# Five small changes in a fused windowed-attention and wave-MLP kernel: value sums, a mixing piece, a weight transpose and a pair of masks put at other places, six fills given to GpSimd

## Chip, cores, metric

The kernel runs on one core of a Trainium2 chip. The metric is the device time of one execution in microseconds (us), lower is better. Times are medians of several executions. All comparisons use fast runs only (runs that are not slowed by a lower TensorE clock; the granted clock is the share of full speed that the profile records for TensorE). A profile is one execution, recorded by the hardware profiler; its span is some 1.8 us shorter than the device time of the same run.

Engine names in the profile: PE is TensorE's matmuls, PEld its weight loads, DVE VectorE, ACT ScalarE, POOL GpSimd, SP the engine that issues most DMA. L267 is line 267 of the kernel file. In the lines by time, the first number is the start in us from the begin of the span, the second the duration in us. Brackets give how long the engine stood idle just before, and what ended that.

## The reference, cut to what matters

```python
# attention: q, k, v are (B=4, H=8, S=768, D=64); 4 sink keys, window of 128
scores = q @ k^T / sqrt(D)
keep   = (key < 4) | ((row - key >= 0) & (row - key < 128))
a      = softmax(where(keep, scores, -1e9))
x      = (a @ v), heads merged: (4, 768, 512)

# wave MLP on x
theta = x @ w_theta
zr, zi = x * cos(theta), x * sin(theta)
u   = x + w_tok_r @ zr + w_tok_i @ zi      # mixing over the 768 tokens
out = u + relu(u @ w_ch)
```

The kernel works on *pairs* of heads, 4 per batch, 16 in all (pair 0 to 3 are batch 0). For one pair: transposes of q and k on PE, three groups of scores (0, 1, 2), exp on ScalarE, a mask product on VectorE for some groups, value sums on PE (called avp or av), division on VectorE (x_nat), transposes of x (xtp). Once a batch of x is there: theta sums (thp), sines on ScalarE (cs), products zz on VectorE, mixing sums (yp) by pieces of three matmuls, u, transposes of u, channel sums (wp), output. While batch b does attention, batch b-1 does its mixing, as filler. In batch 0 there is no filler, and the mixing weights themselves must be transposed on PE (wtp) before they can be used.

## The kernel before: the parts concerned

The order of TensorE, ScalarE, GpSimd and of the DMA queue is the order of the program text; VectorE's is left to a scheduler for batch 0 and is the text's order from batch 1 on.

```python
cast   = pool("cast", 2)                       # q, k in bf16, two buffers each
ps_sc  = pool("ps_sc", 2, space=PSUM)          # scores, thetas: two buffers
ps_sm  = pool("ps_sm", 2, space=PSUM)          # all transposes: two buffers
ps_mm  = pool("ps_mm", 2, space=PSUM)          # mixing and channel sums, first value sums
...
def later_constants():                         # cleared places for later sink values
    nc.vector.memset(vsf, 0.0)                 # 128 x 1024 fp32
    nc.vector.memset(rows, 0.0)
    for tb in range(NB):
        nc.vector.memset(rows[32 * tb:32 * tb + NS, tb:tb + 1], 1.0)
...
# batch 0
for i in range(HP):                            # HP = 4 pairs
    scores(i, 0)
    if i < HP - 1:
        next_heads(i, "q")                     # transposes of the next pair's q
    if i >= 2:
        weigh(i - 2, 0)                        # value sums of a pair, first head
    scores(i, 1)
    if i < HP - 1:
        next_heads(i, "k")
    if i >= 2:
        weigh(i - 2, 1)
    scores(i, 2)
    cast_v(i)                                  # GpSimd: v to bf16
...
wtok_transposes(0, 1)
cast_qk(HP)
mix(0, 0, 0, 4)                                # first mixing sums of block 0
thetas(0, 2)
wtok_transposes(1, 0)                          # weights of block 1
wtok_transposes(1, 1)
cast_wtok(2)
pool_copy(wch[:, 0:2, :], wch_f[0])            # GpSimd: channel weights to bf16
pool_copy(wch[:, 2:4, :], wch_f[1])
...
mix(0, 1, 10, 12)
mixed.append((0, 1))
turn()                                         # transposes of u, block 0
next_heads(HP, "q")
finish()                                       # channel sums and output, block 0
# batch 1
def slot(i, blk, wtok=None):
    ...
    if first:
        ...
        piece(blk, 0)                          # three mixing matmuls of block blk
        piece(blk, 1)
    ...                                        # scores, transposes, more pieces
    if hp > 0:
        weigh(i - 1, 0)
        weigh(i - 1, 1)
    finish()
...
# end of batch 1 (i = 7, its last pair)
five = (p, 5)
mask_product(i, 1)                             # VectorE: two products on E
mask_product(i, 2)
piece(five, 0)
x_transposes(b, HP - 2)                        # third part of x
next_heads(i, "q")
piece(five, 1)
weigh(i, 0)                                    # needs both masks
next_heads(i, "k")
weigh(i, 1)
theta_sums(b, 0, (0, 1))
x_transposes(b, HP - 1)                        # fourth part of x
```

The softmax here doesn't subtract the row's maximum and nothing guards it: scores larger than these inputs give would overflow.

## Time and profile before

| kernel before | |
|---|---|
| device time, median of 4 runs | 184.84 us (184.02 to 185.56) |
| span of the profile | 182.6 us |
| PE busy | 168.3 us, 92% |
| PE idle at the four waits that the change names | 2.50 us |

The chain of work that ended last, in the kernel before (start, duration, what):

```profile
5.57 9.20 DMA vf<-in_v_dram
14.85 1.24 POOL vx L76
16.13 0.50 PE avp L267 x11
```

The values of pair 0 land at 14.8, GpSimd casts them, and only then do the value sums go. ScalarE feels it too, since the next scores stand behind those sums:

```profile
17.43 1.02 ACT L231 ACTIVATE E<-sc 128x1024 bf16<-128x1024 f32 x1 [1.52 <-PE sc L218]
```

### The profile page before, as it was taken

To read this page: it belongs to the slowest core of one execution; us is meant where nothing else is said; L and a number is where in the kernel's file an instruction comes from. 1 tells how busy PE (TensorE), PEld (TensorE's weight loads), DVE (VectorE), ACT (ScalarE), POOL (GpSimd) and SP (SyncE) were. 2 spreads that over 40 slices of the span, in tenths; PEclk is the share of its full clock that TensorE was granted. 3 is DMA by queue.
4 is the path that set the end of the run, shared out by engine and by line. 5 is a ranking of instruction groups with operands and counts; after the bars stand their busy time and mean duration, and the time that the engine had idled before them with its cause. 6 is when DMAs were issued, how large, how long until landed. Compare 5 with 4: busy or idle time off the path is not lost.

```text
span 182.6 us, 4057 instructions
## 1 busy us (share of the span) xinstructions
PE 168.3 (92%) x1617; PEld 90.3 (49%) x1643; DVE 119.8 (66%) x221; ACT 103.0 (56%) x112; POOL 70.6 (39%) x95
## 2 busy tenths in 40 slices
PE   7897997998999988998999999999999999999991
PEld 2444573553466666443565554434555544344560
DVE  6686776792758589377596892686868825824451
ACT  4796778527886683799956801798454029300000
POOL 8987388987751632315584000563000000000000
PEclk9999999999999999999999999999999999999997
DMA  6999999999993899990839765995574530133413
GB/s 176 311 306 258 349 393 408 384 370 341 340 339 134 216 297 288 212 241 15 160 66 165 168 114 148 282 291 143 130 117 102 129 90 0 57 96 105 140 66 115
DMA packets 69907, 36.81 MB, mean 202 GB/s; under 512 B 57984, under 2 KB 64384, under 8 KB 69888
## 3 DMA queue, kind: packets, MB, share of 16 engines
q1 hardware_dynamic: 68592, 36.38, 72.4%
q0 software_dynamic: 1152, 0.04, 0.6%
q8 instruction: 13, 0.21, 0.5%
q10 hardware_dynamic: 144, 0.13, 0.2%
q14 instruction: 6, 0.05, 0.1%
HBM read 25.82 MB, written 6.29 MB: 176 GB/s over the span
## 4 chain that ended last, share of the span: by engine, by line
PE 64%; ACT 10%; DVE 9%; DMA 8%; issue 4%; SPq 2%; POOL 1%; DVEq 0%; ACTq 0%
PE yp L362 25%; PE thp L320 10%; PE wp L390 9%; PE avp L267 5%; DMA vf<-in_v_dram 5%; PE sc L218 5%; SPq L117 2%; DVE zz L333 2%; ACT cs L330 2%; PE tp L192 2%; ACT cs L329 2%; DMA xT<-x_nat 2%; ACT E L231 2%; PE wtp L347 2%; PE xtp L297 2%
## 5 line engine op out<-in xcount | busy, mean ns | idle before, releaser
L231 ACT ACTIVATE E<-sc 128x1024 bf16<-128x1024 f32 x48 | 47.5, 1028 | 14.7 <-PE sc L218 13.5
L362 PE MATMUL yp<-zz,wiT 128*128 128x512 bf16 x133 | 50.4, 379 | 1.3 <-issue 0.8
L362 PE MATMUL yp<-zz,wrT 128*128 128x512 bf16 x131 | 49.7, 380 | 2.0 <-DVE zz L333 1.7
L333 DVE TENSOR_TENSOR zz<-cs,x_nat 128x1024 bf16<-128x1024 bf16 x24 | 21.0, 913 | 14.6 <-ACT cs L330 14.6
L76 POOL TENSOR_SCALAR q<-qf 128x768 bf16<-128x768 f32 x14 | 13.3, 950 | 42.6 <-DMA qf<-in_q_dram 21.9
L237 DVE TENSOR_TENSOR E<-E,mask 128x768 bf16<-128x768 bf16 (+1 forms) x27 | 23.7, 915 | 2.8 <-ACT E L231 2.2
L366 DVE TENSOR_TENSOR u<-yp,x_nat 128x512 bf16<-128x512 f32 x23 | 15.8, 689 | 12.9 <-PE yp L362 12.1
L390 PE MATMUL wp<-wch,uT 128*128 128x512 bf16 x84 | 22.3, 379 | 0.9 <-DVE uT L383 0.5
L320 PE MATMUL thp<-wth,xT 128*128 128x512 bf16 x93 | 22.5, 379 | 0.3
L393 DVE SCALAR_TENSOR_TENSOR of<-wp,u 128x512 f32<-128x512 f32 x23 | 15.8, 685 | 9.4 <-PE wp L390 8.9
L329 ACT ACTIVATE cs<-thp,half_pi 128x1024 bf16<-128x1024 f32 (+1 forms) x13 | 13.6, 1050 | 14.7 <-PE thp L320 14.6
L362 PEld LDWEIGHTS <-wiT 128*128 128x128 bf16 x138 | 13.5, 98 | 14.9 <-issue 2.0
L362 PEld LDWEIGHTS <-wrT 128*128 128x128 bf16 x138 | 13.5, 98 | 13.3 <-issue 1.7
L267 PEld LDWEIGHTS <-E 128*128 128x128 bf16 x480 | 17.1, 97 | 4.9 <-issue 1.2
L218 PE MATMUL sc<-qT,kT 64*128 64x256 bf16 x192 | 16.6, 264 | 1.8 <-ACT kT L196 0.8
L273 DVE TENSOR_TENSOR x_nat<-avp,rec 128x384 bf16<-128x384 f32 x27 | 15.0, 557 | 0.9
L76 POOL TENSOR_SCALAR vx<-vf 128x768 bf16<-128x768 f32 x16 | 14.0, 883 | 1.9 <-DMA vf<-in_v_dram 1.9
L76 POOL TENSOR_SCALAR k<-kf 128x768 bf16<-128x768 f32 x14 | 12.9, 920 | 4.6 <-issue 2.4
L320 PEld LDWEIGHTS <-xT 128*128 128x128 bf16 x96 | 9.1, 98 | 10.7 <-DVE xT L302 0.6
L218 PEld LDWEIGHTS <-kT 64*128 64x128 bf16 x192 | 6.4, 94 | 15.4 <-issue 11.5
L267 PE MATMUL avp<-vx,E 128*128 128x65 bf16 x297 | 13.2, 193 | 0.7 <-POOL vx L76 0.7
L419 ACT COPY lT<-ltp 128x256 bf16<-128x256 bf16 x2 | 0.7, 372 | 21.2 <-PE ltp L417 21.2
(79 smaller groups left out, 206.6 us busy)
## 6 DMA issues: line engine op xcount, KB each, us to landing
qf<-in_q_dram SPq DMA_DIRECT2D x16, 384.0 KB, 5.6
kf<-in_k_dram SPq DMA_DIRECT2D x16, 384.0 KB, 5.8
vf<-in_v_dram SPq DMA_DIRECT2D x16, 384.0 KB, 4.9
out_dram<-of SPq DMA_DIRECT2D x23, 256.0 KB, 2.4
wf<-in_moe_w_tok_r_dram SPq DMA_DIRECT2D x6, 384.0 KB, 6.6
wf<-in_moe_w_tok_i_dram SPq DMA_DIRECT2D x6, 384.0 KB, 7.8
sqf<-in_moe_w_theta_dram SPq DMA_DIRECT2D x2, 512.0 KB, 6.3
sqf<-in_moe_w_ch_dram SPq DMA_DIRECT2D x2, 512.0 KB, 8.1
```

Of the source, the lines that this page charges most:

```text
L76: nc.gpsimd.tensor_scalar(out=out, in0=in_, scalar1=1.0, scalar2=1.0, op0=ALU.mult, op1=ALU.mult)
L218: nc.tensor.matmul(sc[:, e, 256 * part:256 * part + n], lhsT=kT[r, m * P:(m + 1) * P], rhs=qT[r, m * P:m * P + n], start=not biased, stop= ...
L231: nc.scalar.activation(out=E[:, :, 512 * c:512 * (c + 1)], in_=sc, func=AF.Exp, scale=SCALE)
L237: nc.vector.tensor_tensor(out=E[:, :, r], in0=E[:, :, r], in1=mask2[:, :, r], op=ALU.mult)
L267: nc.tensor.matmul(avp[:, t, :], lhsT=lhsT, rhs=rhs, start=(j == 0), stop=(j == len(seq) - 1), skip_group_check=True)
L320: nc.tensor.matmul(th_t[b, g][:, st, :], lhsT=xT[:, cb, 2 * g + st, :], rhs=wth[:, cb, :], start=(cb == 0), stop=(cb == NC - 1))
L329: nc.scalar.activation(out=cs[:, part, 0, :], in_=thp[:, part, :], func=AF.Sin, bias=half_pi)
L333: nc.vector.tensor_tensor(out=z_t[b][:, 2 * g + st, :, :].rearrange("p o (c n) -> p o c n", c=HP), in0=cs[:, st, :, :].rearrange("p o (c n ...
L362: nc.tensor.matmul(yp, lhsT=wT[i][:, t, sc, :], rhs=z_t[b][:, sc, i, :], start=(j == 0), stop=(j == 2 * NT - 1))
L366: nc.vector.tensor_tensor(out=u.rearrange("p (c n) -> p c n", c=HP), in0=yp.rearrange("p (c n) -> p c n", c=HP), in1=x_t[b][:, :, t, :], o ...
L390: nc.tensor.matmul(wp, lhsT=uT[:, cb, :], rhs=wch[:, cb, :], start=(cb == 0), stop=(cb == NC - 1))
L393: nc.vector.scalar_tensor_tensor(out=of, in0=wp, scalar=0.0, in1=u, op0=ALU.max, op1=ALU.add)
```

## The change

Its intent: put ready work of TensorE in front of work that must wait, in four places, and take some memsets from VectorE.

```diff
--- before.py
+++ after.py
@@ -487,10 +487,10 @@
         nc.vector.memset(low, -30000.0)
 
     def later_constants():
-        nc.vector.memset(vsf, 0.0)
-        nc.vector.memset(rows, 0.0)
+        nc.gpsimd.memset(vsf, 0.0)
+        nc.gpsimd.memset(rows, 0.0)
         for tb in range(NB):
-            nc.vector.memset(rows[32 * tb:32 * tb + NS, tb:tb + 1], 1.0)
+            nc.gpsimd.memset(rows[32 * tb:32 * tb + NS, tb:tb + 1], 1.0)
 
     def make_mask():
         ones = struct.unpack("f", struct.pack("I", 0x3F803F80))[0]
@@ -549,7 +549,8 @@
                 next_heads(i, "q")
             if i >= 3 * HP:
                 scores(i, 0)
-            piece(blk, 0)
+            if i > HP:
+                piece(blk, 0)
             piece(blk, 1)
         if pending:
             wtok_transposes(pending.pop(), 1)
@@ -588,6 +589,9 @@
         if hp > 0:
             weigh(i - 1, 0)
             weigh(i - 1, 1)
+        if i == 2 * HP - 1:
+            mask_product(i, 1)
+            mask_product(i, 2)
         finish()
         if wtok is not None:
             pending.append(wtok)
@@ -624,9 +628,11 @@
         scores(i, 0)
         if i < HP - 1:
             next_heads(i, "q")
-        if i >= 2:
+        if i > 2:
             weigh(i - 2, 0)
         scores(i, 1)
+        if i == 2:
+            weigh(i - 2, 0)
         if i < HP - 1:
             next_heads(i, "k")
         if i >= 2:
@@ -657,9 +663,9 @@
     phases(0, 1)
     wtok_transposes(0, 1)
     cast_qk(HP)
+    wtok_transposes(1, 0)
     mix(0, 0, 0, 4)
     thetas(0, 2)
-    wtok_transposes(1, 0)
     wtok_transposes(1, 1)
     cast_wtok(2)
     pool_copy(wch[:, 0:2, :], wch_f[0])
@@ -681,6 +687,7 @@
     mixed.append((0, 1))
     turn()
     next_heads(HP, "q")
+    piece((0, 2), 0)
     finish()
 
 
@@ -721,8 +728,6 @@
             piece(five, 1)
         else:
             five = (p, 5)
-            mask_product(i, 1)
-            mask_product(i, 2)
             piece(five, 0)
             x_transposes(b, HP - 2)
             next_heads(i, "q")
```

It has five parts, called A to E below. **A**: later sinks cleared by GpSimd. **B**: value sums of pair 0 (its first head) behind pair 2's second scores. **C**: one weight transpose ahead of the first mixing sums. **D**: the first mixing piece of block 2 ahead of the first channel sums (and no longer in slot 4). **E**: masks of pair 7 ahead of the output step of block 4, which stands in `finish()`.

## The prediction, written before the changed kernel ran

> **What bounds the kernel now.** I read the page first, then the chain of work that ended last, then the waits and the instructions in order of time around each line that the diff touches. The page's busy table says that TensorE is the engine to look at, and the slices say that its throttle grants it nearly full speed throughout, so only its idle time and its order matter:
>
> ```profile
> PE 168.3 (92%) x1617; PEld 90.3 (49%) x1643; DVE 119.8 (66%) x221; ACT 103.0 (56%) x112; POOL 70.6 (39%) x95
> PE   7897997998999988998999999999999999999991
> ...
> PE 64%; ACT 10%; DVE 9%; DMA 8%; issue 4%; SPq 2%; POOL 1%; DVEq 0%; ACTq 0%
> ```
>
> PE is 92% busy and holds 64% of the chain. Its thin slices lie in the first 45 us, and the diff works mostly there. In order of time, TensorE waits there at four places that the change names (start, duration, then the idle time before it and its releaser):
>
> ```profile
> 16.13 0.50 PE L267 MATMUL avp<-vx,E 128*128 128x65 bf16 x11 [0.73 <-POOL vx L76]
> ...
> 30.70 0.38 PE L362 MATMUL yp<-zz,wrT 128*128 128x512 bf16 x1 [0.64 <-DVE zz L333]
> ...
> 41.73 1.04 PE L390 MATMUL wp<-wch,uT 128*128 128x512 bf16 x3 [0.46 <-DVE uT L383]
> ...
> 72.15 0.27 PE L267 MATMUL av<-vx,E 128*128 128x65 bf16 x3 [0.67 <-DVE E L237]
> ```
>
> The reader is to see four different waits, all before instructions that the diff moves: the first pair's value sums wait for the GpSimd cast of values that land late; the first mixing sums wait for the products zz; the first channel sums wait for the copy of a transpose; the last pair of batch 1 waits for its mask. Added, they are 2.50 us, 1.4% of the time. What the change can win is about that.
>
> **What the Trainium skill says.** "TensorE: Matmul & The Clock Gate", section "Step-by-step: what each phase is for": only weight loads are pulled ahead, matmuls stay in program order. So a waiting matmul holds all later ones, and moving a ready group in front of it is free. The trace agrees: in the 0.73 us nothing else ran on PE, though the next scores had all they needed (below). "SBUF — State Buffer", section "Who interferes with whom": a VectorE instruction with two SBUF inputs contends with a GpSimd instruction that reads SBUF, and the first to issue blocks the other; one that only writes does not contend. The trace agrees on the first half:
>
> ```profile
> 69.18 0.68 DVE L393 SCALAR_TENSOR_TENSOR of<-wp,u 128x512 f32<-128x512 f32 x1
> 69.78 1.22 DVE L237 TENSOR_TENSOR E<-E,mask 128x2048 bf16<-128x2048 bf16 x1
> ...
> 70.55 1.14 POOL L76 TENSOR_SCALAR q<-qf 128x768 bf16<-128x768 f32 x1 [5.21 <-PE tp L192]
> ...
> 70.91 1.18 DVE L237 TENSOR_TENSOR E<-E,mask 128x768 bf16<-128x768 bf16 x1
> ```
>
> The 128x768 mask product, whose shortest record is 0.55 us, took 1.18 beside that cast, and the cast 1.14 instead of 0.83. "GPSIMD Engine Reference", section "3. Performance versus the Vector engine", warns that GpSimd is slower per element; for a memset this case's own 128x704 fill took 0.68 us, and that is what I use.
>
> **Part by part.**
>
> *Later sinks cleared by GpSimd.* VectorE loses a memset of 0.91 us at 4.34, one of 0.06 and four small ones (0.37). It gains no time on the path: after them it waits 1.16 us for the second query's DMA anyway, and the first scores at 7.99 follow ScalarE, which starts the mask's bias at 5.08 when GpSimd has made the mask, then copies qT and kT until 7.93. An earlier cast of k changes neither. GpSimd gets 1024/704 x 0.68 = 0.99 us, plus five small fills (those at the start are issued 0.03 us apart but last 0.10): about 1.3 us. They go behind the fourth value cast, which ends at 19.82, where GpSimd idles 2.10 us until a weight lands at 21.92. Hidden. **0 us.**
>
> *Value sums of pair 0 behind the second scores of pair 2.* Before, PE ends the transposes of pair 3's q at about 15.12, issues four sink products, waits to 16.13, does the sums and starts those scores at 16.47. They need a scores buffer whose exp ended near 14.9 (three exps start at 12.85, 1.02 each), so they can start at 15.12. They last 0.86 us (16.47 to 17.32) and end at 15.98; the cast of the values ends at 16.09; so the sums start with practically no wait. Everything behind them gains 0.73. ScalarE gains more at once: its exp waited 1.52 us until 17.43 and can now start when the exp before it ends, 15.91, plus some 0.1. VectorE takes up kT of pair 3 about 0.5 us sooner, which just keeps pace with the scores that need it. Later suppliers have slack: the third and fourth values are cast by 19.82 and used after 22; the theta weights by 24.27 and needed at 25.9. **0.7 us.**
>
> *A weight transpose ahead of the first mixing sums.* Six transposes, 0.34 us, leave a busy stretch at 34.1 and go into the 0.64 us wait. The compiled order shows VectorE's copy of it (0.47) now between the second product and the third, where VectorE waits 0.45 for ScalarE. But the gain is not all kept: at 37.19 the next weight transpose needs the PSUM buffer that ScalarE's copy of qT frees at 36.99, only 0.20 earlier; that copy follows the sines of the third theta group, which does not come earlier by this part. So 0.34 shrinks to about **0.15 us**.
>
> *A mixing piece ahead of the first channel sums.* Three matmuls of 0.216 spacing, 0.65 us, go into a wait that the trace gives as 0.46; counting the pipelined tail of the transposes before it (six at 0.056 from 40.77 end their issue at 41.11), PE stands for 0.62. The piece fills it; the channel sums start where they did, and the piece is gone from behind them. Its sum buffer is free once the first u is formed (40.48). **0.6 us.**
>
> *Masks of pair 7 ahead of the output of block 4.* VectorE swaps one 0.60 us step with two mask products. PE's 0.67 wait goes, but PE then meets VectorE again at 74.12, where the last transposes of x wait for x_nat. VectorE runs without a pause from 69.18 to 74.07, and a swap inside does not shorten that. What does is the contention: the small product would run from 70.3 to 70.9, starting before the cast at 70.55, and keep its 0.55 instead of 1.18. That is **0.6 us** if the order of issue turns so, and 0.05 if not; I take 0.45.
>
> Sum: 0 + 0.7 + 0.15 + 0.6 + 0.45 = **1.9 us**. Behind it the waits are mostly relative (PE, ScalarE and VectorE waiting for each other), and the loads have slack: the casts in batch 1 wait for PE's transposes to free a buffer more than for DMA. So I expect most to reach the end, and take 0.1 off for a wait that reforms: 184.6 - 1.8 = **182.8 us**.
>
> **Rivals.**
> - *VectorE is the bound at the end of batch 1.* Then the mask swap gives 0.05 and only some 1.4 us remain: 183.2. For it: VectorE's unbroken run to 74.07, while PE arrives at 74.10. Against it: the contended 1.18.
> - *Transfers bound the first batch.* DMA engines are over 90% busy in nearly all slices to 50 us. If the value and weight loads set the pace, the first gain is handed back and the total is about 0.8: 183.8. Against it: casts of q, k and weights for batch 1 end 4 to 10 us ahead of their transposes.
> - *A new wait takes the place of an old one.* With the mixing piece ahead, channel sums of block 1 take the buffer that u of block 2 must leave; u begins at 46.81 and lasts 0.69, and those sums start at 47.5 to 47.7. That is even, worth 0.2 at most. GpSimd's fills could delay the weights if each took several times the estimate: 0.8 us of slack stand against it.
> - *Everything is kept, and contention falls elsewhere too* (zz lasts 1.30 beside a cast, 0.84 alone): 182.0.
>
> **Range and chances.** The rivals span 182.0 to 183.8. The three runs before span 1.5 us, so medians may be off by 0.4 on either side: 181.8 to 184.0. Faster by over 2% needs 180.9, more than the four waits together: 4%. Slower by over 2% would need 3.7 us of new waits, for which I see no cause: 1%. Within 2%: 95%.
>
> **What would show it.** Right: value sums of pair 0 near 16.0 with no wait of 0.7, ScalarE's idle 1.52 gone; x transposes near 21.5 instead of 22.21; the first channel sums near 40.9 with no wait, mixing right behind; av without its 0.67, and a 128x768 mask near 0.55; theta sums of batch 1 starting about 1.9 earlier than 73.30 to 75.28. Wrong: the value sums still waiting for GpSimd; a weight wait longer than 2.10 or moved behind the fills; PE waiting about 0.6 for x_nat near 73; an end that moved much less than the start of batch 2 did.

## More of the kernel before

Since TensorE keeps its order within each kernel, the run can be cut into six stretches by the starts of seven PE instructions. The busy time by stretches of the kernel before (first two numbers: the stretch and its length; then busy us and count of PE, PEld, DVE, ACT and POOL; then the granted clock, the DMA share and GB/s):

```profile
core 0: us, PE busy (x) PEld busy (x) DVE busy (x) ACT busy (x) POOL busy (x), PEclk, DMA share, GB/s
7.99:22.21 14.22, 12.60 (x189) 6.86 (x193) 10.76 (x23) 10.94 (x11) 9.52 (x13) 1.00 1.12 306
22.21:41.73 19.52, 17.62 (x197) 10.96 (x191) 15.24 (x25) 12.10 (x16) 17.69 (x19) 1.00 1.06 387
41.73:43.99 2.26, 2.21 (x9) 0.89 (x10) 0.69 (x1) 1.65 (x2) 2.26 (x3) 1.00 1.15 348
43.99:69.56 25.57, 24.14 (x309) 14.89 (x314) 16.96 (x32) 18.88 (x22) 11.90 (x16) 1.00 0.90 273
69.56:74.12 4.56, 3.82 (x55) 2.65 (x54) 4.41 (x8) 2.06 (x3) 2.36 (x3) 1.00 1.16 279
74.12:178.71 104.59, 101.37 (x843) 51.22 (x857) 66.20 (x112) 52.38 (x55) 19.60 (x22) 1.00 0.57 131
```

The cuts are: first scores; first transposes of x; first channel sums; first scores of batch 1; third part of x of batch 1; fourth part of x; last matmuls. Idle PE is small everywhere, and the waits that the change names lie in the first, second, third and fifth stretch. (PE counts differ by a few between profiles, since some matmul records are missing from a trace; starts are not affected.)

## The result

| | before | changed |
|---|---|---|
| first measurement, median | 184.84 us, 4 runs | 182.30 us, 4 runs (182.03 to 182.62) |
| second measurement, on chip 10 | 184.82 us, 11 runs | 182.49 us, 5 runs (181.72 to 182.62) |
| ratio, first | | 0.9864, 95% interval 0.9818 to 0.9910 |
| ratio, second | | 0.9853, 95% interval 0.9822 to 0.9885 |

A ratio is the mean time of the changed kernel's fast runs over that of the other kernel's fast runs of the same rounds, so it is not quite the ratio of the medians. The change gains 1.4 to 1.5%, about 2.5 us: clear of noise. The point prediction was 182.8.

The stretches of the changed kernel's first profile, by the same seven instructions:

```profile
8.01:21.45 13.44, 13.01 (x193) 6.83 (x193) 10.36 (x19) 10.97 (x11) 10.55 (x16) 1.00 1.11 295
21.45:40.83 19.38, 18.38 (x201) 11.11 (x194) 15.44 (x25) 12.13 (x16) 17.21 (x20) 1.00 1.06 386
40.83:42.44 1.61, 1.61 (x9) 0.59 (x9) 0.55 (x1) 1.59 (x2) 1.42 (x3) 1.00 1.14 328
42.44:68.00 25.56, 24.57 (x314) 14.87 (x314) 17.55 (x33) 18.93 (x23) 14.81 (x18) 1.00 0.97 297
68.00:71.94 3.94, 3.77 (x56) 2.56 (x55) 3.79 (x8) 2.35 (x3) 2.52 (x3) 1.00 0.69 175
71.94:176.41 104.47, 102.70 (x856) 51.20 (x857) 66.11 (x112) 52.12 (x55) 19.54 (x22) 1.00 0.62 136
```

Stretch by stretch the gain is 0.78, 0.14, 0.65, 0.01, 0.62 and 0.12 us, 2.32 in all, less 0.02 for a later start: 2.30, which is the difference of the spans (182.6 and 180.3). The four places of the prediction, in the changed kernel's lines by time:

```profile
16.15 1.02 ACT L231 ACTIVATE E<-sc 128x1024 bf16<-128x1024 f32 x1 [0.17 <-PE sc L218]
16.20 0.50 PE L267 MATMUL avp<-vx,E 128*128 128x65 bf16 x11
...
29.68 0.38 PE L362 MATMUL yp<-zz,wrT 128*128 128x512 bf16 x1
...
40.83 1.03 PE L390 MATMUL wp<-wch,uT 128*128 128x512 bf16 x4
...
69.44 0.50 PE L267 MATMUL av<-vx,E 128*128 128x65 bf16 x11
```

None of the four has an idle time ahead of it any more, and ScalarE's 1.52 us are 0.17. What TensorE now waits for in batch 0 between 25 and 42 us is this:

```profile
30.91 0.38 PE L362 MATMUL yp<-zz,wrT 128*128 128x512 bf16 x1 [0.37 <-DVE zz L333]
34.84 0.39 PE L362 MATMUL yp<-zz,wiT 128*128 128x512 bf16 x1 [0.30 <-DVE wiT L351]
```

The first was there before. The second is new: a wait for VectorE's copy of the other weight transpose, which stood behind two products zz. It takes back part of what the transpose moved into the first wait had gained; the second stretch gained only 0.14 in this profile (more under "C alone").

The masks of part E, with the cast that disturbed them before:

```profile
67.63 1.68 DVE L237 TENSOR_TENSOR E<-E,mask 128x2048 bf16<-128x2048 bf16 x2
68.76 0.55 DVE L237 TENSOR_TENSOR E<-E,mask 128x768 bf16<-128x768 bf16 x1
68.99 1.01 POOL L76 TENSOR_SCALAR q<-qf 128x768 bf16<-128x768 f32 x1 [5.23 <-PE tp L192]
```

Before, both mask products together took 2.31 us. The small one (the second line, which is the tail of the first) now starts 0.23 us before the cast and takes 0.55 instead of 1.18; the cast is the one that is lengthened.

And the fills of part A on GpSimd:

```profile
19.09 1.23 POOL L76 TENSOR_SCALAR vx<-vf 128x768 bf16<-128x768 f32 x1 [0.58 <-DMA vf<-in_v_dram]
20.27 0.94 POOL L490 MEMSET vsf<- 128x1024 f32 x1
21.16 0.09 POOL L491 MEMSET rows<- 128x4 f32 x1
21.31 0.48 POOL L493 MEMSET rows<- 4x1 f32 x4
21.87 2.06 POOL L76 TENSOR_SCALAR wth<-sqf 128x1024 bf16<-128x1024 f32 x2
```

They take 1.52 us, and the weight casts follow at once. GpSimd did not wait for the weights' DMA here, so they may have landed before the fills ended. Nothing was lost, since the theta sums that use the first weights start at 24.67.

### The profile page after: what moved, and what is told of

Its sections match the earlier page's. It is cut to its first block, busy times and chain, and to the rows that moved or that the text cites.

```text
span 180.3 us, 4084 instructions
## 1 busy us (share of the span) xinstructions
PE 169.7 (94%) x1643; PEld 89.4 (50%) x1643; DVE 118.5 (66%) x215; ACT 103.1 (57%) x112; POOL 73.3 (41%) x101
## 4 chain that ended last, share of the span: by engine, by line
PE 66%; ACT 15%; DVE 8%; DMA 3%; issue 2%; POOL 2%; DVEq 0%; ACTq 0%; POOLq 0%
PE yp L362 25%; PE wp L390 9%; PE thp L320 9%; PE sc L218 6%; PE avp L267 6%; ACT E L231 3%; ACT cs L329 3%; ACT cs L330 3%; DVE zz L333 3%; PE tp L192 3%; DMA xT<-x_nat 2%; PE sc L211 2%; PE wtp L347 2%; PE xtp L297 2%; DVE x_nat L273 1%
## 5 line engine op out<-in xcount | busy, mean ns | idle before, releaser
L362 PE MATMUL yp<-zz,wrT 128*128 128x512 bf16 x138 | 52.4, 380 | 0.9 <-DVE zz L333 0.6
L362 PE MATMUL yp<-zz,wiT 128*128 128x512 bf16 x138 | 52.3, 379 | 0.6 <-DVE wiT L351 0.3
L390 PE MATMUL wp<-wch,uT 128*128 128x512 bf16 x92 | 23.6, 379 | 0.1
L76 POOL TENSOR_SCALAR k<-kf 128x768 bf16<-128x768 f32 x14 | 13.6, 970 | 4.6 <-DMA kf<-in_k_dram 2.5
```

Source lines behind the costliest of these rows:

```text
L76: nc.gpsimd.tensor_scalar(out=out, in0=in_, scalar1=1.0, scalar2=1.0, op0=ALU.mult, op1=ALU.mult)
L362: nc.tensor.matmul(yp, lhsT=wT[i][:, t, sc, :], rhs=z_t[b][:, sc, i, :], start=(j == 0), stop=(j == 2 * NT - 1))
L390: nc.tensor.matmul(wp, lhsT=uT[:, cb, :], rhs=wch[:, cb, :], start=(cb == 0), stop=(cb == NC - 1))
```

## The experiments

Twelve runs were made, of eleven kernels (the changed one and ten variants). Each was correct and was timed in five rounds beside the kernel before on the same chip. The medians below come from three chips, so the ratios are what can be compared. Since the fast runs of one kernel span 0.6 to 2.6 us (in the profiles, part of it is when the first loads land), the totals of parts worth 0.6 us have wide intervals. The stretches of the profiles are the sharper instrument, because each part lies in one stretch. All profiles of fast runs, with the length of stretches 1 to 6 in us:

| kernel (parts in it) | first scores at | 1 | 2 | 3 | 4 | 5 | 6 | median us | ratio to before (95%) |
|---|---|---|---|---|---|---|---|---|---|
| before | 7.99 | 14.22 | 19.52 | 2.26 | 25.57 | 4.56 | 104.59 | 184.8 | 1 |
| b_only (B) | 7.99 | 13.39 | 19.32 | 2.27 | 25.56 | 4.57 | 104.63 | 183.49 | 0.9950 (0.9916 to 0.9984) |
| c_only (C) | 7.99 | 14.23 | 19.00 | 2.27 | 25.56 | 4.57 | 104.60 | 183.95 | 0.9956 (0.9930 to 0.9982) |
| d_only (D) | 8.87 | 14.13 | 19.52 | 1.60 | 25.57 | 4.57 | 104.60 | 184.58 | 0.9984 (0.9956 to 1.0011) |
| e_only (E) | 7.99 | 13.87 | 19.48 | 2.26 | 25.57 | 3.94 | 104.47 | 184.21 | 0.9962 (0.9939 to 0.9985) |
| no_e (ABCD) | 8.01 | 13.39 | 18.86 | 1.60 | 25.57 | 4.57 | 104.65 | 182.87 | 0.9921 (0.9886 to 0.9957) |
| no_e_cast3 | 8.01 | 13.92 | 19.35 | 1.61 | 25.89 | 4.50 | 104.47 | 183.25 | 0.9939 (0.9900 to 0.9978) |
| no_e_dve10 | 8.01 | 13.60 | 18.81 | 1.61 | 25.66 | 3.87 | 104.65 | 182.82 | 0.9889 (0.9844 to 0.9934) |
| changed (ABCDE) | 8.01 | 13.44 | 19.38 | 1.61 | 25.56 | 3.94 | 104.47 | 182.30 | 0.9864 (0.9818 to 0.9910) |
| after_again (ABCDE) | 8.01 | 13.57 | 18.82 | 1.61 | 25.57 | 3.93 | 104.60 | 182.49 | 0.9853 (0.9822 to 0.9885) |
| split_act2 | 8.02 | 13.63 | 19.20 | 1.61 | 25.70 | 3.93 | 104.45 | 182.23 | 0.9854 (0.9821 to 0.9887) |
| wch_act | 8.02 | 14.22 | 19.37 | 1.60 | 25.56 | 3.93 | 104.65 | 182.95 | 0.9886 (0.9849 to 0.9924) |

### B alone

```diff
+        if i > 2:
             weigh(i - 2, 0)          # was: if i >= 2
         scores(i, 1)
+        if i == 2:
+            weigh(i - 2, 0)
```

> Only the value sums of pair 0 are moved behind pair 2's second scores; the rest is the kernel before. Theory (the wait for the late value cast is filled, and every later step in the first batch follows): 0.7 to 0.8 us faster, 183.9 to 184.1 against 184.8; in the trace the value sums start near 16.2 without a wait, the first x transposes near 21.5 instead of 22.2, the last transposes of x in batch 1 near 73.4 instead of 74.1. Rival (transfers set the pace of the first batch): the start gains and the gain is gone by 45 us; the time stays at 184.8.

The value sums start at 16.13 without a wait, the first x transposes at 21.38 instead of 22.21, and the fourth part of x of batch 1 at 73.10 instead of 74.12. So the gain of the first stretch is not handed back by 45 us: the rival that transfers set the pace of batch 0 falls. Stretch 1 shrinks by 0.83. The table also shows a limit: without B, stretch 1 was 14.22, 14.23, 14.13, but 13.87 in e_only, where the value cast came earlier (14.27) and the sums started at 15.77; and with B it was 14.22 in wch_act, where the sums still waited:

```profile
16.99 0.50 PE L267 MATMUL avp<-vx,E 128*128 128x65 bf16 x11 [0.49 <-POOL vx L76]
```

B is worth what the late values cost in a given run, up to the 0.86 us of scores that it puts in front.

### C alone

```diff
+    wtok_transposes(1, 0)
     mix(0, 0, 0, 4)
     thetas(0, 2)
-    wtok_transposes(1, 0)
     wtok_transposes(1, 1)
```

> Only the weight transpose is moved ahead of the first mixing sums. Theory of the prediction (a PSUM buffer that ScalarE frees binds behind it): 0.15 us faster. Second theory, from the trace after (the products zz and the copy of the other weight transpose on VectorE bind behind it, not the PSUM buffer): 0.0 to 0.2 us faster, with a PE wait for the copy of a weight transpose near 35. Rival (the whole 0.34 is kept): 0.34 us faster. Told apart in the trace by how much earlier the first channel sums (41.73 before) start, and by what PE waits for between 33 and 38.

The channel sums start at 41.22 instead of 41.73, and stretch 2 shrinks by 0.52: more than the whole 0.34 of the rival, and the total (0.8 us by the ratio, interval 0.3 to 1.3) agrees. The wait for the copy near 35 is there, 0.30 us at 35.26. So none of the three expectations fits as it stands. Part of the reason shows when the products zz and GpSimd's casts are set side by side. In the second profile of the changed kernel the first zz started with no cast running, in its first profile and in the kernel before a cast ran already (zz starts, and the casts near it):

```profile
28.72 0.69 DVE L333 TENSOR_TENSOR zz<-cs,x_nat 128x1024 bf16<-128x1024 bf16 x1 [0.31 <-ACT cs L330]
28.72 1.38 POOL L76 TENSOR_SCALAR q<-qf 128x768 bf16<-128x768 f32 x1 [0.17 <-DMA qf<-in_q_dram]
```

```profile
28.26 0.83 POOL L76 TENSOR_SCALAR q<-qf 128x768 bf16<-128x768 f32 x1 [0.18 <-DMA qf<-in_q_dram]
28.57 1.05 DVE L333 TENSOR_TENSOR zz<-cs,x_nat 128x1024 bf16<-128x1024 bf16 x1 [0.32 <-ACT cs L330]
```

```profile
29.27 0.83 POOL L76 TENSOR_SCALAR k<-kf 128x768 bf16<-128x768 f32 x1
29.34 1.30 DVE L333 TENSOR_TENSOR zz<-cs,x_nat 128x1024 bf16<-128x1024 bf16 x1 [0.31 <-ACT cs L330]
```

```profile
28.66 0.83 POOL L76 TENSOR_SCALAR q<-qf 128x768 bf16<-128x768 f32 x1 [0.22 <-DMA qf<-in_q_dram]
29.35 0.69 DVE L333 TENSOR_TENSOR zz<-cs,x_nat 128x1024 bf16<-128x1024 bf16 x1 [0.32 <-ACT cs L330]
```

In order, the fences are the second profile of the changed kernel, its first, the kernel before, and c_only. Where zz is first it takes 0.69 us and the cast is lengthened; where the cast is first, zz takes 1.05, and 1.30 in the kernel before, whose cast of k started 0.07 us ahead of zz. In c_only the cast of q is recorded as having 0.14 us left when zz starts, and zz still takes 0.69 (times on GpSimd are rough), so it is counted with the runs in which zz is ahead. Which comes first depends on when a load lands: the cast of q waited for its DMA in each of these four runs. Counting only runs of the same kind, C is worth this in stretch 2: zz ahead, 19.32 (b_only) against 19.00 (c_only), 18.86, 18.82 and 18.81 with C, that is 0.32 to 0.51; cast ahead, 19.52, 19.48 and 19.52 against 19.38 (changed), 19.35 and 19.37 (two kernels that differ a little otherwise), that is 0.10 to 0.17. By this comparison, of the 0.52 of C alone 0.20 (19.52 to 19.32) goes with the order of zz and cast, which is luck, and 0.32 with C, close to the 0.34 of the rival. Each kernel has one profile, so these are differences of single runs.

In b_only one sees what C took away in the first case. There the two weight transposes of block 1 stand in a row, fill both PSUM buffers for transposes, and the next transposes wait for VectorE's copy:

```profile
34.20 0.49 PE L192 MATMUL tp<-ident,q 128*128 128x128 bf16 x6 [0.51 <-DVE wrT L351]
```

With C they no longer stand in a row. In the kernel before, the chain of work that ended last goes through the same copy (DVE wrT at 34.61) before the transposes at 35.23.

### D alone

```diff
     next_heads(HP, "q")
+    piece((0, 2), 0)
     finish()
 ...
-            piece(blk, 0)
+            if i > HP:
+                piece(blk, 0)
```

> Only the mixing piece is put ahead of the first channel sums. Theory (it fills PE's standing time of 0.62 us): 0.6 us faster; the channel sums still start near 41.73, the first scores of batch 1 near 43.35 instead of 43.99, the last transposes of x in batch 1 near 73.5 instead of 74.12. Rival (the buffer of the sums is freed later and a wait forms at the channel sums of block 1): under 0.4 us, with a PE wait near 47.

Stretch 3 is 1.60 instead of 2.26, a gain of 0.66 that appears alike in every kernel with D (1.60 or 1.61) and in none without it. No wait formed near 47. The rival falls. The total does not show it: 0.9984 with an interval that holds both 0 and 0.66 us. In the profiled run the first scores started 0.88 us late, at 8.87, because the first keys landed late. VectorE's cast of them, at 5.22 in the kernel before, had to wait for their DMA:

```profile
6.54 0.56 DVE L137 CAST k<-kf 128x768 bf16<-128x768 f32 x1 [1.29 <-DMA kf<-in_k_dram]
```

D does not touch anything before that point, so this is a difference between runs, and it covers the gain. Whether the other runs of this kernel had the same late start isn't known, since only one was profiled.

### E alone

```diff
             weigh(i - 1, 1)
+        if i == 2 * HP - 1:
+            mask_product(i, 1)
+            mask_product(i, 2)
         finish()
 ...
-            mask_product(i, 1)
-            mask_product(i, 2)
```

> Only the masks of pair 7 are put ahead of the output of block 4. Theory (contention: the small mask product starts before GpSimd's cast and keeps 0.55 us instead of 1.18): 0.6 us faster, the small mask product near 0.55 us, the last transposes of x in batch 1 near 73.5 instead of 74.12. Rival (VectorE's chain is only reordered): under 0.1 us faster with those transposes still near 74.1, though PE's wait of 0.67 for the mask is gone.

Stretch 5 is 3.94 instead of 4.56, by 0.62, and both mask products together take 1.68 us. The rival (order alone) expected about 4.5 or more. Since the edit changes the order and the contention at once, this alone does not say which of them did it; three further kernels were made for that.

### A alone

The edit is the first hunk of the diff.

> Only the later sinks are cleared by GpSimd. Theory (hidden on both engines): same time, within 0.1 us of the kernel before; the first scores still at 8.0, the fills on GpSimd between 19.8 and 21.3 and the first weight cast still near 21.9. Rival (VectorE's memsets were on the path, or the fills delay the weights): the first scores or the theta sums (25.44 before) move by 0.3 us or more.

0.9991, interval 0.9956 to 1.0027, medians of the fast runs 184.60 with A and 184.48 without: nothing to see. Its profile fell in a slow run (granted clock 0.845, 200.5 us) and is not used. That A costs nothing shows in stretch 1, 13.39 both with A (no_e) and without it (b_only). First scores are at 7.99 without A and at 8.01 with it.

### E taken away from the changed kernel

> The changed kernel with the masks of pair 7 back behind the output of block 4. Theory: it loses 0.6 us against the changed kernel (182.9 against 182.3), the small mask product takes about 1.18 us again beside the cast of q. Rival (order alone): it loses under 0.1.

Stretch 5 is back at 4.57, the small mask product back at 1.18 us. The total lost is 0.4 to 0.6 us by the medians (182.87 against 182.49 and 182.30, on different chips) and 0.6 to 0.7%, 1.0 to 1.3 us, by the ratios, whose intervals overlap. The stretch is the better measure.

### A test of contention that did not test it

```diff
-    cast = pool("cast", 2)
+    cast = pool("cast", 3)            # and E taken away
```

> As the run before, but the casts of q and k have three buffers instead of two, so GpSimd need not wait for the transposes of pair 8 and does its next cast earlier; VectorE's order is the old one. Theory (contention): the small mask product of pair 7 falls back to about 0.55 us although the output still goes first, and the last transposes of x in batch 1 start about 0.6 us earlier than in the run before: 182.3. Rival (the order of output and masks is what counts): those transposes stay, 182.9. Other contention may move by 0.3 us either way, so the place itself in the trace decides, not the total.

The cast of pair 10 did move away, to 64.22, but it was replaced. With one more buffer, the cast of pair 11 is released by the very transposes that released pair 10's, and it starts at 69.76, between the two masks:

```profile
69.76 1.08 POOL L76 TENSOR_SCALAR q<-qf 128x768 bf16<-128x768 f32 x1 [1.85 <-PE tp L192]
70.07 1.18 DVE L237 TENSOR_TENSOR E<-E,mask 128x768 bf16<-128x768 bf16 x1
```

The small product still took 1.18 us, and stretch 5 stayed at 4.50. By the words of the expectation this is the rival's result, but the cause was not taken away, so it decides nothing. It shows that one more buffer moved this collision by a whole step: the same release started the cast of another pair. At its new place the cast of pair 10 took 1.79 us beside other mask products, and stretch 4 grew to 25.89.

### A test of contention that did

```diff
-    CASTS = {..., ("k", 1): "dve"}
+    CASTS = {..., ("k", 1): "dve", ("q", 10): "dve"}   # and E taken away
```

> The third buffer of the run before did not do what it was made for: another cast ran beside the small mask product again. Here VectorE's order is the old one (output before masks of pair 7), and only the one cast of q (pair 10) that GpSimd does beside those masks is given to VectorE some 10 us later. Theory (contention): the small mask product of pair 7 takes 0.55 us, and from the transposes of x's third part to those of its fourth, which took 4.57 us in the old order and 3.94 in the new, it takes about 3.95. Rival (the order is what counts): 4.57 again. The total is not decisive, since VectorE has 0.6 us more to do later.

With the old order on VectorE (output first, then masks) and no cast beside them:

```profile
68.98 0.55 DVE L237 TENSOR_TENSOR E<-E,mask 128x768 bf16<-128x768 bf16 x1
```

The small product takes 0.55 us and stretch 5 is 3.87, against 4.57 in no_e and 3.93 with E. So the whole gain of part E is the avoided contention. The order of output and masks counts only because it makes the mask start ahead of the cast. Next to no_e one instruction moved (the cast ran on VectorE at 81.89), and its old stretch lost 0.70 us.

### The changed kernel once more

> The changed kernel once more, on the chip of the candidates: about 1.2 to 1.4% faster than the kernel before. From the first x transposes to the first channel sums it took 19.38 us in its first profile and 18.86 in the kernel without the mask part, which is the same program up to there. Theory (where GpSimd's casts meet VectorE's zz varies from run to run): either figure, or one between. Rival (the difference is fixed): 19.38.

18.82 in stretch 2, with zz at 0.69: the theory of a run-to-run difference holds, and the first profile had an unlucky meeting. By the ratio the kernel is 1.5% faster, a little more than expected. The medians of the two measurements (182.30, 182.49) differ little.

### Two candidates to beat both

The first (run twice, as split_act and split_act2, the same kernel):

```diff
     wtok_transposes(1, 0)
-    mix(0, 0, 0, 4)
-    thetas(0, 2)
+    mix(0, 0, 0, 2)
     wtok_transposes(1, 1)            # copied by ScalarE now
+    mix(0, 0, 2, 4)
+    thetas(0, 2)
```

> A candidate to beat both: the changed kernel with the other weight transpose of block 1 also put into a wait, between the second and third mixing sums (PE waits 0.37 us there), and copied by ScalarE, which idles then, instead of VectorE. Theory (VectorE's products zz and this copy bind PE near 34.8): the 0.30 us wait for the copy goes and 0.34 us of transposes lie in a wait; 0.3 to 0.6 us faster than the changed kernel, 181.8. Rival (products zz bind the later mixing sums anyway, or the ScalarE copy delays the sines): same as the changed kernel within 0.1.

Its profile fell in a run of 332.64 us, in which matmuls went at half rate from begin to end. The five other runs were fast, 181.44 to 184.03 with a median of 182.3; the ratio, 0.9908 (0.9856 to 0.9960), does not tell it from the changed kernel.

> The candidate of the call before again, whose profile fell in a run at half matmul rate and shows nothing. Theory: the wait for the copy of a weight transpose near 35 is gone, from the first x transposes to the first channel sums it takes 18.5 to 18.9 us; 0.3 to 0.5 us faster than the changed kernel on the same chip. Rival (the products zz bind there): 18.9 to 19.4 and the same time.

Beside the changed kernel on one chip: 182.23 and 182.49, ratios 0.9854 and 0.9853, the same. Stretch 2 took 19.20, which is within the rival's 18.9 to 19.4. The waits at 30.91 and 34.84 are gone, but a new one took their place:

```profile
36.29 0.50 PE L347 MATMUL wtp<-ident,raw 128*128 128x128 bf16 x6 [0.41 <-POOL q L76]
```

The profile names GpSimd, but by the times it is another: the transposes need a PSUM buffer, and that is freed by ScalarE's copy of qT, which starts at 35.44 and lasts 0.80, so ends at 36.24. This is the wait that the prediction had expected in part C; it became the bound only here, where what stands ahead of it came earlier.

The second:

```diff
-    pool_copy(wch[:, 0:2, :], wch_f[0])
-    pool_copy(wch[:, 2:4, :], wch_f[1])
 ...
     next_heads(HP - 1, "k")
+    nc.scalar.copy(out=wch[:, 0:2, :], in_=wch_f[0])
+    nc.scalar.copy(out=wch[:, 2:4, :], in_=wch_f[1])
```

> A second candidate: the changed kernel with the two casts of the channel weights (2.8 us of GpSimd beside the products zz) given to ScalarE, in a stretch where it idles 3.1 us. Theory (those casts lengthen zz, 2.76 us for two in the first profile): two zz near 1.7 to 2.2 us, from the first x transposes to the first channel sums 18.9 or less, up to 0.5 us faster than the changed kernel. Rival (other casts move up and collide instead, or ScalarE comes too late for the channel sums): same time or slower.

By the time the rival is right: 182.95 against 182.49, no faster, and stretch 2 is 19.37. The first half of the theory did come true: the two zz after the second theta group take 0.74 and 1.31, together 1.97 instead of 2.76. Why this didn't shorten the stretch stays open. The loads landed late in this profile (GpSimd waited 1.58 us for mixing weights until 27.41), and the first zz took 1.27 beside the cast of those weights, so it is no clean comparison. Neither candidate beats the changed kernel, which stays the best.

## Why the prediction was right

The measured 182.3 lies in the range and 0.5 us under the point. That closeness is partly luck: the forecast took 1.8 us off a base of 184.6, while the gain was 2.5 us from a median of 184.84, so a gain that was 0.7 too small and a base that was 0.24 too low partly cancelled. Step by step:

- **A, 0 us: right.** The fills took 1.52 us where 1.3 was estimated; the four small ones took 0.48 instead of some 0.2. In the first profile of the changed kernel they used up the wait for the weights, and it cost nothing because the theta sums come later still.
- **B, 0.7 us: right.** 0.83 alone, 0.78 in the changed kernel, and it reached the end. Its size is set by when the values land: in a run with an early landing there was less to win (13.87 without B), in a late one B did not cover the wait.
- **C, 0.15 us: the size failed.** It was 0.10 to 0.17 where GpSimd's cast was ahead of zz, and 0.32 to 0.51 where zz was ahead. The step "0.34 shrinks to about 0.15" rested on a wait for ScalarE's copy of qT near 37. With C alone and in the changed kernel TensorE did not stand there; in the second profile of the changed kernel that copy ended at 35.76, just ahead of the transposes at 35.84. What stood in the way in the first profile and in c_only was the 0.30 us wait for the copy of the other weight transpose behind the products zz. What enlarged the gain where zz was ahead was not in the prediction at all: two transposes in a row fill both buffers, and the next group waits for a copy (0.51 us in b_only). The prediction also read a zz of 0.84 as one alone. GpSimd cast mixing weights beside it, from 30.22 to 32.56, and undisturbed it takes 0.69.
- **D, 0.6 us: right.** 0.65 or 0.66 in stretch 3 of every profile with D. That it reaches the total isn't shown by D alone.
- **E, 0.6 if the mask comes ahead of the cast, taken as 0.45: right in mechanism, and the bet was too careful.** All profiles with E gave 0.62 or 0.63, because the margin that was estimated from the records of before, 0.25 us (70.3 and 70.55), turned out as 0.23. The rival that VectorE is the bound there fits as well: stretch 5 has 3.79 us of VectorE work in 3.94. So only a shorter VectorE instruction, not a swap, could help, as the old order without the cast shows (3.87).
- **"Most to reach the end, and 0.1 off for a wait that reforms": nothing came off.** Stretch 4 is 25.56 or 25.57 in all kernels but three (25.66 to 25.89, in no_e_cast3, no_e_dve10 and split_act2), and stretch 6 is between 104.45 and 104.65, whatever happened before. The 0.12 that stretch 6 gained in the first profile belongs to no part. That the engines there wait for each other and not for a load, so that a gain only shifts them, fits this, but no run tested it.

The sum of the five single parts by ratios is 1.6% (2.9 us), a little more than the 1.4 to 1.5% of all together, well within their intervals. What stays open is whether late loads explain the small gain of all runs of d_only, or only of the one that was profiled.

## What to carry to other kernels

Where an in-order engine is the bound, list its waits by time and look for ready work just behind each; the gain of a move is the wait, less what the moved work meets at its new place. Behind a wait there is often a second one (here a PSUM buffer, a copy or a contended product) that takes over when the first is removed, so each part is best judged by the length of its own stretch, not by the total. And where a VectorE instruction with two inputs in SBUF runs beside a cast on GpSimd, ask which of the two starts first: an order of steps that changes nothing in the sum of work can be worth the 0.6 us by which a late starter is held up, and a cast that is moved away can be replaced by the next in line, as with the third buffer.

## What the Trainium skill lacked or had wrong

- "SBUF — State Buffer", section "Who interferes with whom", states the rule that decided part E and that the runs bear out: who issues first keeps the port. It lacks how this looks in a profile: the recorded duration holds the time of being blocked. The same 128x768 mask product is recorded as 0.55 us or 1.18, the first product zz as 0.69 to 1.30, the cast of q beside it as 0.83 or 1.38.
- "TensorE: Matmul & The Clock Gate", section "Back-to-back issue gap", gives about 131 ns per matmul of 512 columns as the sustained rate of load and matmul pairs. Here 18 such pairs in a row took 3.88 us in the chain of both kernels, 0.216 us each, which is that section's figure for an isolated matmul. No profile of a fast run has 512-column matmuls closer than some 0.2 us.
- The same page, "What's actually happening", has TensorE leave its slow clock after some 3.4 us of sustained work. In one run of split_act, matmuls of 512 columns followed each other at 0.44 to 0.47 us (four channel matmuls in 1.89), twice the usual 0.216, and stayed so from begin to end, with PE 98% busy over 330.8 us. The column for the granted clock says 1.00, but the summary of that profile has no clock line and its trace no clock record (the others have two or more), so the 1.00 is no measurement. That TensorE never left its slow clock fits the rate and isn't shown. That section has no such case, and it did not come back in the repeat.
- "GPSIMD Engine Reference" gives no time for a memset. Here a 128x1024 fp32 fill took 0.94 us on GpSimd and 0.91 on VectorE, and four fills of 4x1 took 0.48 us together on GpSimd and 0.37 on VectorE. So the large fill is nearly as fast there, while a cast of 128x768 from fp32 to bf16 took 0.83 us on GpSimd and 0.56 on VectorE.
